# Planning VectorE steps with two SBUF inputs around GpSimd, in the experts of an attention and mixture-of-experts kernel

## The chip, the core and the metric

One core of one Trainium2 chip. The metric is device time in microseconds (us) from the first to the last instruction of one execution, all outputs being written to HBM. Engines are TensorE (PE in the profile's rows), VectorE (DVE), ScalarE (ACT), GpSimd (POOL) and SyncE (SP), which issues the DMAs. Each engine works off its own queue in order.

## What is computed

Clustered attention over 4 batches and 8 heads (768 rows of 64), and a dense mixture of 8 experts on its output, 3072 tokens by 512. Only the second half is touched by the change:

```python
logits = x @ w_gate                      # x: 3072 x 512, 8 experts
P = np.exp(logits - logits.max())
for _ in range(8):                       # rows and columns of P normalised in turn
    ...
for e in range(8):
    h = np.maximum(x @ w1[e], 0.0)       # 512 -> 1024
    out += P[:, e:e+1] * (h @ w2[e])     # 1024 -> 512
```

All is float32 to the outside. The expert products are done in float16 pairs: each operand is split into a high half and the rest, and three products of halves are added up.

## The kernel before

**Stages.** Attention fills the first 490 us. The experts follow, in 64 units of work; a unit is one batch (768 tokens), one expert and one half of that expert's hidden columns, and has two halves of 256 columns each. The first units are (batch 0), (batch 1), (batch 1), (batch 0), then batch 2 twice and batch 3 twice, all of expert 0. So unit 4 is the first that needs the x tiles of batch 2, and unit 6 those of batch 3.

**One half of a unit.** The first layer is a 2x2 block scheme with seven products in place of eight (`layer1`, lines 1493 to 1522), each of six matmuls of 128x384. They are accumulated in three PSUM tiles, `a_ps`, `b_ps` and `c_ps`. In between, partial results are copied out: ScalarE makes `c11`, `c22`, `c12` and `h21` (line 1529, functions `c_11`, `c_22`, `c_12`, `sums_of`), and TensorE's next product into the same PSUM tile waits for that copy: the second product of `a_ps` for c11, the second of `c_ps` (operand B22) for c22, the third of `a_ps` (operand T3) for c12. VectorE then adds the second product from PSUM (line 1532, one SBUF input). From these come seven operands of the second layer: c12, c22 and c11 through a relu (`split_raw`: ScalarE line 1538, VectorE line 1540), and four sums s1, h21, s2 (kept in c22) and s4 (kept in c12), made on VectorE by `relu_with` (line 1623, two SBUF inputs) and split by `split_sum` (ScalarE's cast, line 1547, and a subtraction, line 1549, on GpSimd or VectorE). Each of the tiles c11, c12, c22, h21 and s1 has two buffers; the c22 buffer comes back when s4 has read it and s2 is split, that of c12 when s4 is split.

**Second layer.** `layer2` multiplies the operands with the second weights into three PSUM banks (line 1693), and VectorE adds the results to the accumulators (lines 1727, 1729, 1733). The first three batches are added up for expert 0 without a gate and scaled by it afterwards on ScalarE (line 1744).

**Beside it** run the gates (lines 1195 to 1251, with tiny matmuls, line 1239), the making of the weight operands (`make_first`, lines 1302 to 1321, and `make_second`, lines 1341 to 1360; 4 subtractions and 3 splits each on GpSimd or VectorE), the scan of the next expert's weights for their largest value (line 323 on VectorE, then two DMAs through HBM, lines 274 and 277), and the x tiles of batches 2 and 3 (`next_x`): load (line 1408), for batch 3 a largest value and its round trip, scaling (line 1425), four subtractions (line 338), seven splits (line 1437), store (line 1440) and load for the unit (line 1471).

**The order** is written by a planner in the program (`Planner`, lines 62 to 166). Each piece of work is a generator that yields an engine and a duration before it issues its instructions; the planner keeps a time for each engine, begins the step that can start first (within a patience of 0.1 us the one with the smallest due time), and fixes each engine's order as planned. A step may name two engines, `either` (line 1275), and is then given to the one that can begin first, VectorE with a handicap of 0.3 or 1.5 us. The names in `PORT`, `"POOL"` and `"DVE*"`, share one more time, `self.port`: such a step starts only when the last one of either kind has ended. Attention's steps already use `"DVE*"`; the experts' used plain `DVE`, which knows nothing of GpSimd. The plan's times set the order alone; on the chip semaphores rule.

Of the kernel before, what the change touches and what calls it, by code (L numbers as in the profile page):

```python
# [171 lines left out]
def attn_moe_kernel(  # L172
# [63 lines left out]
    PE, ACT, DVE, POOL, SP = "PE", "ACT", "DVE", "POOL", "SP"  # L236
# [113 lines left out]
    with ExitStack() as actx:  # L350
# [178 lines left out]
        ev = Events()  # L529
# [623 lines left out]
    FULL = NG2 * B  # L1153
# [25 lines left out]
    ev = Events()  # L1179
# [8 lines left out]
    def urgent(t):  # L1188
        plan.now.key = lead + t
# [85 lines left out]
    def either(pool, dve, alone=False):  # L1275
        if alone:
            return (POOL, pool)
        return (POOL, pool), (DVE, dve, 0.3 if ev["slot", FULL].time is None else 1.5)

    def raw_tile():  # L1280
        return rawp.tile([P, 1024], F32, name="raw")
# [5 lines left out]
    def make_first(e, f2):  # L1287
# [18 lines left out]
        for o, a, b_, op in ((0, (0, 0), (0, 1), ALU.add), (1, None, (1, 0), ALU.subtract), (2, (1, 0), (0, 0), ALU.subtract), (3, (1, 1), None, ALU.subtract)):  # L1306
            w = yield either(0.82, 0.4, e == 0 and f2 < 2)
            if o == 0:
                sums = sump.tile([P, 1024], F32, name="sums")
                S_ = sums.rearrange("p (o c f) -> p o c f", o=4, c=KC)  # L1310
            x = S_[:, 0] if a is None else A[:, a[0], a[1]]
            y = S_[:, 1] if b_ is None else A[:, b_[0], b_[1]]
            by(w).tensor_tensor(out=S_[:, o], in0=x, in1=y, op=op)
        yield ACT, 0.4
        t = wa[e, f2] = wap.tile([P, 2, 7, KC, P], F16, name="wa")
        for o, a, cost in ((slice(A22, A22 + 1), A[:, 0, 1:2], 0.4), (slice(A11, A12 + 1), A[:, 1], 0.61), (slice(S1, S4 + 1), S_, 1.04)):
            if cost > 0.4:
                yield ACT, cost
            nc.scalar.copy(t[:, 0, o], a)
            w = yield either(2 * cost, 1.15 * cost, e == 0 and f2 < 2)  # L1320
            by(w).tensor_tensor(out=t[:, 1, o], in0=a, in1=t[:, 0, o], op=ALU.subtract)
# [4 lines left out]
    def make_second(e, f2):  # L1326
# [18 lines left out]
        for o, a, b_, op in ((0, (0, 1), (0, 0), ALU.subtract), (1, None, (1, 1), ALU.subtract), (2, (1, 1), (0, 1), ALU.subtract), (3, (1, 0), None, ALU.add)):  # L1345
            w = yield either(0.82, 0.4, e == 0 and f2 < 2)
            if o == 0:
                sums = sump.tile([P, 1024], F32, name="sums")
                T_ = sums.rearrange("p (o f) -> p o f", o=4)
            x = T_[:, 0] if a is None else Bk[:, a[0], a[1]]  # L1350
            y = T_[:, 1] if b_ is None else Bk[:, b_[0], b_[1]]
            by(w).tensor_tensor(out=T_[:, o], in0=x, in1=y, op=op)
# [171 lines left out]
    def k_tile(k, name):  # L1524
        t = kt[k, name] = cp.tile([P, HB], F32, name=name)
        return t

    def scaled(t, ps, func=AF.Copy):
        nc.scalar.activation(t, ps[:, 0:HB], func, scale=KAPPA)  # L1529
# [4 lines left out]
    def split_raw(k, o, c):  # L1534
        yield t_h
        yield ACT, 0.522
        t = h[k, o] = hp.tile([P, 2, HB], F16, name="h")
        nc.scalar.activation(t[:, 0], c, AF.Relu)  # L1538
        yield DVE, 0.607
        nc.vector.scalar_tensor_tensor(out=t[:, 1], in0=c, scalar=0.0, in1=t[:, 0], op0=ALU.max, op1=ALU.subtract)  # L1540
        ev["h", k, o].set(plan)

    def split_sum(k, o, c):
        yield t_h
        yield ACT, 0.522
        t = h[k, o] = hp.tile([P, 2, HB], F16, name="h")
        nc.scalar.copy(t[:, 0], c)  # L1547
        w = yield either(0.95, 0.54)
        by(w).tensor_tensor(out=t[:, 1], in0=c, in1=t[:, 0], op=ALU.subtract)  # L1549
        ev["h", k, o].set(plan)  # L1550

    def c_12(k, t):
        yield ev["p", k, 2]
        yield t_k["c12"]
        urgent(t + 6)
        yield ACT, 0.49
        c = k_tile(k, "c12")
        scaled(c, ps1[k, "a"])
        ev["u2", k].set(plan)
        yield ev["p", k, 3]  # L1560
        urgent(t + 8)
        yield DVE, 0.555
        plus(c, ps1.pop((k, "c")))
        t_c.put(plan)
        ev["c12", k].set(plan)
        urgent(t + 14)
        yield from split_raw(k, "A12", c)

    def c_22(k, t):
        yield ev["p", k, 1]  # L1570
        yield t_k["c22"]
        urgent(t + 4)
        yield ACT, 0.49
        c = k_tile(k, "c22")
        scaled(c, ps1[k, "c"])
        ev["m5", k].set(plan)
        yield ev["p", k, 4]
        urgent(t + 10)
        yield DVE, 0.555
        plus(c, ps1[k, "a"])  # L1580
        ev["c22", k].set(plan)
        urgent(t + 15)
        yield from split_raw(k, "A11", c)
# [18 lines left out]
    def freed(name, *events):  # L1602
        for x in events:
            yield x
        t_k[name].put(plan)

    def sums_of(k, t):
        yield ev["p", k, 6]
        yield t_k["h21"]
        urgent(t + 14)  # L1610
        yield ACT, 0.49
        h21 = k_tile(k, "h21")
        scaled(h21, ps1.pop((k, "a")), AF.Relu)
        t_a.put(plan)
        yield ev["c11", k]
        yield t_k["s1"]
        urgent(t + 17)
        yield DVE, 0.58
        s_1 = k_tile(k, "s1")
        c11, c12, c22 = (kt[k, n] for n in ("c11", "c12", "c22"))  # L1620

        def relu_with(out_, c, other, op):
            nc.vector.scalar_tensor_tensor(out=out_, in0=c, scalar=0.0, in1=other, op0=ALU.max, op1=op)  # L1623

        relu_with(s_1, c11, h21, ALU.add)
        ev["s1", k].set(plan)
        plan.spawn(freed("c11", ev["s1", k], ev["h", k, "A22"]), lead + t)
        plan.spawn(split_sum(k, "S1", s_1), lead + t + 18)
        urgent(t + 20)
        yield DVE, 0.58  # L1630
        relu_with(h21, c22, h21, ALU.subtract)
        plan.spawn(split_sum(k, "S3", h21), lead + t + 26)
        plan.spawn(freed("h21", ev["h", k, "S3"]), lead + t)
        yield ev["h", k, "A11"]
        urgent(t + 20)
        yield DVE, 0.58
        relu_with(c22, c22, s_1, ALU.subtract)
        ev["s2", k].set(plan)
        plan.spawn(split_sum(k, "S2", c22), lead + t + 22)
        plan.spawn(freed("s1", ev["s2", k], ev["h", k, "S1"]), lead + t)  # L1640
        yield ev["h", k, "A12"]
        urgent(t + 24)
        yield DVE, 0.58
        relu_with(c12, c12, c22, ALU.add)
        ev["s4", k].set(plan)
        plan.spawn(split_sum(k, "S4", c12), lead + t + 28)
        plan.spawn(freed("c22", ev["s4", k], ev["h", k, "S2"]), lead + t)
        plan.spawn(freed("c12", ev["h", k, "S4"]), lead + t)
# [171 lines left out]
```

## Time and profile before

| | us |
|---|---|
| median of 3 runs (2294.29 to 2296.83) | 2295.07 |
| profiled execution: span from first to last instruction | 2294.3 |
| TensorE busy, share of the span | 2233.1, 97% |
| VectorE busy | 1859.2, 81% |
| GpSimd busy | 1408.1, 61% |
| ScalarE busy | 1161.5, 51% |

The page gives no other time for the profiled execution than its span, which agrees with the lowest of the runs. Busy times are summed durations; a VectorE instruction that is held up after its start counts as busy. The page's chain of waits, followed back from the end, is TensorE for 88% of the span, VectorE for 5% and others for the rest. What TensorE waits for stands in the rows below.

### The profile page before, as it was taken

The numbers are of one execution on the slowest core, as the hardware profiler recorded it, in microseconds if no ns is written. First come the engines' busy times: TensorE is split into PE (matmuls) and PEld (weight loads), VectorE is DVE, ScalarE is ACT, GpSimd is POOL, SyncE is SP. The second block draws the span as 40 slices with busy tenths as digits, with TensorE's granted clock in tenths as the row PEclk, the third lists the DMA queues.
The fourth block names the chain that finished last, engine by engine and source line by source line (L and its number), as shares of the span: only waits on it lengthen the run. The fifth ranks groups of instructions, "written<-read, shape, count | busy, mean of one in ns | idle before, by whom it ended". The sixth has DMA issues, their size and how long they took to land.

```text
span 2294.3 us, 43174 instructions
## 1 busy us (share of the span) xinstructions
PE 2233.1 (97%) x16190; PEld 1606.9 (70%) x16190; DVE 1859.2 (81%) x3544; ACT 1161.5 (51%) x2324; POOL 1408.1 (61%) x1385
## 2 busy tenths in 40 slices
PE   7999999988989999999999999999999999999998
PEld 4666666546767777777777777777777777777777
DVE  7887877779977987788779877987797789777776
ACT  4565656656555545454535453545454444445432
POOL 5887878878755756464737473747465655556431
PEclk7999999999999999999999999999999999999999
DMA  7675554544521524152426232523343253414242
GB/s 159 158 164 146 136 139 112 160 165 152 184 91 72 180 79 141 57 189 90 141 64 198 70 115 86 170 79 107 121 137 113 71 162 96 134 49 135 61 138 78
DMA packets 178010, 281.03 MB, mean 122 GB/s; under 512 B 64596, under 2 KB 101384, under 8 KB 177288
## 3 DMA queue, kind: packets, MB, share of 16 engines
q1 hardware_dynamic: 177800, 278.27, 41.3%
q8 instruction: 127, 2.08, 0.4%
q14 instruction: 83, 0.68, 0.1%
HBM read 225.82 MB, written 23.69 MB: 109 GB/s over the span
## 4 chain that ended last, share of the span: by engine, by line
PE 88%; DVE 5%; POOL 2%; ACT 2%; issue 2%; DMA 1%; SPq 0%; DVEq 0%; POOLq 0%; ACTq 0%
PE a_ps L1509 20%; PE a_ps L1693 14%; PE ac_ps L1693 12%; PE c_ps L1693 10%; PE c_ps L1509 10%; PE b_ps L1509 5%; PE av_ps L900 5%; PE max_ps L767 3%; PE exp_ps L838 3%; PE exp_ps L839 2%; DVE mrt L771 1%; PE misc_ps L626 1%; ACT pe L845 1%; PE misc_ps L938 1%; PE misc_ps L662 0%
## 5 line engine op out<-in xcount | busy, mean ns | idle before, releaser
L1693 PEld LDWEIGHTS <-h 128*128 128x128 f16 x8064 | 789.9, 98 | 192.6 <-issue 7.6
L1509 PEld LDWEIGHTS <-wa 128*128 128x128 f16 x5376 | 526.7, 98 | 278.6 <-issue 17.3
L1549 POOL TENSOR_TENSOR h<-s,h 128x384 f16<-128x384 f32 x127 | 124.8, 983 | 541.0 <-ACT h L1547 530.3
L1538 ACT ACTIVATE h<-c 128x384 f16<-128x384 f32 x384 | 200.5, 522 | 437.3 <-DVE c L1532 435.8
L1693 PE MATMUL a_ps<-wb,h 128*128 128x256 f16 x3072 | 377.2, 273 | 0.7 <-DVE acc L1733 0.6
L1693 PE MATMUL ac_ps<-wb,h 128*128 128x256 f16 x2688 | 367.3, 273 | 1.0 <-DVE acc L1729 1.0
L1693 PE MATMUL c_ps<-wb,h 128*128 128x256 f16 x2304 | 284.2, 273 | 3.9 <-DVE acc L1729 2.8
L1733 DVE SCALAR_TENSOR_TENSOR acc<-a_ps,gates,acc 128x256 f32<-128x256 f32 x460 | 215.1, 479 | 88.7 <-PE a_ps L1693 85.9
L867 POOL TENSOR_TENSOR psum<-psum,pe 128x512 f32<-128x512 f32 (+1 forms) x240 | 247.9, 1056 | 43.1 <-ACT pe L845 40.1
L1549 POOL TENSOR_TENSOR h<-c,h 128x384 f16<-128x384 f32 x252 | 249.3, 1001 | 27.6 <-ACT h L1547 26.5
L1540 DVE SCALAR_TENSOR_TENSOR h<-c,h 128x384 f16<-128x384 f32 x384 | 255.2, 668 | 6.8 <-ACT h L1538 6.7
L1733 DVE SCALAR_TENSOR_TENSOR acc<-ac_ps,gates,acc 128x256 f32<-128x256 f32 x402 | 192.2, 478 | 34.0 <-PE ac_ps L1693 31.6
L771 DVE TENSOR_REDUCE mrt<-max_ps 128x1 f32<-128x512 f32 (+1 forms) x288 | 188.5, 683 | 38.1 <-PE max_ps L767 36.5
L1733 DVE SCALAR_TENSOR_TENSOR acc<-c_ps,gates,acc 128x256 f32<-128x256 f32 x344 | 155.8, 477 | 74.9 <-PE c_ps L1693 74.4
L1529 ACT ACTIVATE c<-a_ps 128x384 f32<-128x384 f32 x256 | 125.1, 489 | 162.6 <-PE a_ps L1509 162.4
L845 ACT ACTIVATE pe<-exp_ps 128x512 f32<-128x512 f32 x288 | 166.5, 598 | 68.6 <-PE exp_ps L839 60.2
L1547 ACT CAST h<-c 128x384 f16<-128x384 f32 x256 | 128.2, 509 | 81.4 <-DVE c L1623 81.1
L1549 POOL TENSOR_TENSOR h<-h,h 128x384 f16<-128x384 f32 x124 | 140.4, 1132 | 36.0 <-PE c_ps L1693 23.9
L900 PE MATMUL av_ps<-pe,vn 128*64 128x512 f32 (+1 forms) x768 | 132.7, 491 | 0.0
L767 PE MATMUL max_ps<-kX,qX 96*128 96x256 f32 (+1 forms) x384 | 120.6, 385 | 10.8 <-DVE mrt L771 5.5
L839 PE MATMUL exp_ps<-qX,kX 98*128 98x512 f32 (+1 forms) x384 | 126.1, 340 | 0.0
L1529 ACT ACTIVATE h<-a_ps 128x384 f32<-128x384 f32 x128 | 62.7, 490 | 111.8 <-PE a_ps L1509 111.6
(472 smaller groups left out, 3916.7 us busy)
## 6 DMA issues: line engine op xcount, KB each, us to landing
raw<-in_moe_w SPq DMA_DIRECT2D x120, 512.0 KB
qn<-in_q SPq DMA_DIRECT2D x16, 384.0 KB
kn<-in_k SPq DMA_DIRECT2D x16, 384.0 KB
qX<-qH SPq DMA_DIRECT2D x32, 192.0 KB
kX<-kH SPq DMA_DIRECT2D x32, 192.0 KB
vn<-in_v SPq DMA_DIRECT2D x8, 768.0 KB
xd<-xT SPq DMA_DIRECT2D x4, 1536.0 KB
xqB<-xd SPq DMA_DIRECT2D x16, 384.0 KB
```

The costliest lines, as they stand in the source:

```text
L767: nc.tensor.matmul(ps[:, y * (z - a) : (y + 1) * (z - a)], t["qa"][0:96, i * P : (i + 1) * P], t["k2"][0:96, a:z], start=True, stop=True)
L771: nc.vector.tensor_reduce(out=t["mr"][:, i0 : i0 + ni, ni - 1], in_=ps.rearrange("p (x c) -> p x c", x=ni), axis=AX, op=ALU.max)
L845: nc.scalar.activation(pe, ps.rearrange("p (x c) -> p x c", x=ni), AF.Exp, scale=SCALE)
L867: (nc.gpsimd if w == POOL else nc.vector).tensor_tensor(out=st[:, a:z], in0=old[a], in1=part, op=ALU.add)
L900: nc.tensor.matmul(av[o, a:z], vn[:, i, :], heads[t]["pe", c][:, i - i0], start=(i == 0), stop=False, skip_group_check=True)
L1509: nc.tensor.matmul(ps[:, 0:HB], wt[:, w_, a, c, :], xv[:, x_, c, :], start=(n in (0, 1, 5) and s_ == 0), stop=(s_ == len(steps) - 1), skip ...
L1529: nc.scalar.activation(t, ps[:, 0:HB], func, scale=KAPPA)
L1538: nc.scalar.activation(t[:, 0], c, AF.Relu)
L1540: nc.vector.scalar_tensor_tensor(out=t[:, 1], in0=c, scalar=0.0, in1=t[:, 0], op0=ALU.max, op1=ALU.subtract)
L1549: by(w).tensor_tensor(out=t[:, 1], in0=c, in1=t[:, 0], op=ALU.subtract)
L1693: nc.tensor.matmul(view(m, i), t[:, a_, i * P : (i + 1) * P], w[:, b_, x, :], start=(opens and n == 0 and i in (0, 2)), stop=(n == 5), ski ...
L1733: nc.vector.scalar_tensor_tensor(out=to, in0=src, scalar=gate[b, e][:, ti : ti + 1], in1=to, op0=ALU.mult, op1=ALU.add)
```

## The change

Five places in the experts' plan name `"DVE*"` in place of `DVE`: the two-engine steps of `either`, the VectorE half of `split_raw`, and the four relu sums of `sums_of`. No duration, due time or instruction is altered, but the order of ScalarE, VectorE, GpSimd and SyncE in the experts comes out differently, and the choice between two engines.

```diff
     def either(pool, dve, alone=False):
         if alone:
             return (POOL, pool)
-        return (POOL, pool), (DVE, dve, 0.3 if ev["slot", FULL].time is None else 1.5)
+        return (POOL, pool), ("DVE*", dve, 0.3 if ev["slot", FULL].time is None else 1.5)
...
         nc.scalar.activation(t[:, 0], c, AF.Relu)
-        yield DVE, 0.607
+        yield "DVE*", 0.607
         nc.vector.scalar_tensor_tensor(out=t[:, 1], in0=c, scalar=0.0, in1=t[:, 0], op0=ALU.max, op1=ALU.subtract)
...
         urgent(t + 17)
-        yield DVE, 0.58
+        yield "DVE*", 0.58
         s_1 = k_tile(k, "s1")
...
         urgent(t + 20)
-        yield DVE, 0.58
+        yield "DVE*", 0.58
         relu_with(h21, c22, h21, ALU.subtract)
...
         urgent(t + 20)
-        yield DVE, 0.58
+        yield "DVE*", 0.58
         relu_with(c22, c22, s_1, ALU.subtract)
...
         urgent(t + 24)
-        yield DVE, 0.58
+        yield "DVE*", 0.58
         relu_with(c12, c12, c22, ALU.add)
```

In the whole program 12 steps go from VectorE to GpSimd: nine of line 1549, one each of lines 1313, 1321 and 1437. TensorE's order differs only in where the small matmuls of line 1239 stand.

**Place A, unit 1, first half.** ScalarE, from the copy of c11 to that of c12; numbers tell the buffers apart, and c22_6094, c12_6105 and h21_6149 (below) belong to unit 0's first half. Before:

```order
L1529 ACTIVATE c11_6276<-a_ps_6248 128x384
L1547 CAST h_6281<-s1_6274 128x384
L1529 ACTIVATE c22_6286<-c_ps_6267 128x384
L1538 ACTIVATE h_6291<-c11_6166 128x384
L1302 ACTIVATE raw_6097<-raw_6097,s1_93 128x1024
L1547 CAST h_6301<-c22_6179 128x384
L1547 CAST h_6313<-h21_6257 128x384
L1222 ACTIVATE pr_6015<-lg_80,gneg_6311 128x24x8
L1529 ACTIVATE c12_6317<-a_ps_6248 128x384
```

Now:

```order
L1529 ACTIVATE c11_6279<-a_ps_6240 128x384
L1547 CAST h_6282<-h21_6149 128x384
L1547 CAST h_6292<-c22_6094 128x384
L1547 CAST h_6297<-s1_6294 128x384
L1222 ACTIVATE pr_6015<-lg_80,gneg_6299 128x24x8
L1547 CAST h_6306<-c12_6105 128x384
L1529 ACTIVATE c22_6309<-c_ps_6256 128x384
L1547 CAST h_6324<-h21_6252 128x384
L1425 ACTIVATE xqB11_6250<-xqB11_6250,sx_96 128x768
L1529 ACTIVATE c12_6331<-a_ps_6240 128x384
```

The copies of c22 and c12 now stand behind casts of unit 0's sums. On VectorE these sums come, before the change, in one run:

```order
L1623 SCALAR_TENSOR_TENSOR s1_6164<-c11_6086,h21_6150 128x384
L1623 SCALAR_TENSOR_TENSOR h21_6150<-c22_6094,h21_6150 128x384
L1202 TENSOR_REDUCE gmax_6181<-lg_80 128x1
L1623 SCALAR_TENSOR_TENSOR c22_6094<-c22_6094,s1_6164 128x384
L1623 SCALAR_TENSOR_TENSOR c12_6105<-c12_6105,c22_6094 128x384
```

and now with nine other steps between (these rows and the sum into c12_6105, which follows):

```order
L1623 SCALAR_TENSOR_TENSOR s1_6195<-c11_6086,h21_6149 128x384
L1532 SCALAR_TENSOR_TENSOR c12_6189<-c_ps_6151,c12_6189 128x384
L1532 SCALAR_TENSOR_TENSOR c22_6171<-a_ps_6141,c22_6171 128x384
L1532 SCALAR_TENSOR_TENSOR c11_6165<-b_ps_6212,c11_6165 128x384
L1211 TENSOR_REDUCE g1_6247<-g_ps_6210 1x1
L1540 SCALAR_TENSOR_TENSOR h_6158<-c11_6086,h_6158 128x384
L1623 SCALAR_TENSOR_TENSOR h21_6149<-c22_6094,h21_6149 128x384
L1540 SCALAR_TENSOR_TENSOR h_6219<-c12_6189,h_6219 128x384
L1623 SCALAR_TENSOR_TENSOR c22_6094<-c22_6094,s1_6195 128x384
L1540 SCALAR_TENSOR_TENSOR h_6225<-c22_6171,h_6225 128x384
L1623 SCALAR_TENSOR_TENSOR s1_6294<-c11_6165,h21_6252 128x384
L1219 TENSOR_SCALAR gneg_6299<-g_ps_6271 128x1
```

The sums of unit 0's first half have moved behind the three combinations from PSUM (line 1532) and four other steps of its second half.

**Place B, unit 3, second half** (the first half is alike). ScalarE, from c11 to c12, before:

```order
L1529 ACTIVATE c11_7035<-a_ps_7011 128x384
L1435 CAST xt2T2_7051<-xqB11_6259 128x768
L1529 ACTIVATE c22_7069<-c_ps_7040 128x384
L1547 CAST h_7072<-s1_7049 128x384
L1529 ACTIVATE c12_7088<-a_ps_7011 128x384
```

Now:

```order
L1529 ACTIVATE c11_7188<-a_ps_7173 128x384
L1435 CAST xt2T2_7201<-xqB11_6250 128x768
L1435 CAST xt2B22_7241<-xqB22_6273 128x768
L1547 CAST h_7245<-h21_6967 128x384
L1547 CAST h_7250<-c22_6834 128x384
L1435 CAST xt2T3_7259<-xqB12_6266 128x768
L1547 CAST h_7265<-c12_6858 128x384
L1529 ACTIVATE c22_7267<-c_ps_7194 128x384
L1435 CAST xt2B21_7294<-xqB21_6269 128x768
L1529 ACTIVATE c12_7302<-a_ps_7173 128x384
```

The copy of c22 has moved behind the casts of the earlier half's h21, c22 and c12 and two more tiles of batch 2.

**Place C, unit 4, first half.** ScalarE around the scalings of line 1744. Before, they stand behind the copy of c12 and the splits of its tiles:

```order
L1529 ACTIVATE c22_7449<-c_ps_7428 128x384
L1529 ACTIVATE c12_7474<-a_ps_7392 128x384
L1547 CAST h_7477<-h21_7389 128x384
L1547 CAST h_7489<-c22_7250 128x384
L1547 CAST h_7501<-c12_7274 128x384
L1538 ACTIVATE h_7512<-c12_7474 128x384
L1538 ACTIVATE h_7536<-c22_7449 128x384
L1744 ACTIVATE acc111_6772<-acc111_6772,gates_7534 128x256 x2
L1744 ACTIVATE acc122_6884<-acc122_6884,gates_7534 128x256 x2
```

Now:

```order
L1529 ACTIVATE c22_7471<-c_ps_7413 128x384
L1744 ACTIVATE acc111_6738<-acc111_6738,gates_7476 128x256 x2
L1744 ACTIVATE acc122_6840<-acc122_6840,gates_7476 128x256 x2
L1744 ACTIVATE acc121_7008<-acc121_7008,gates_7476 128x256 x2
L1744 ACTIVATE acc111_6738<-acc111_6738,gates_7476 128x256
L1744 ACTIVATE acc122_6840<-acc122_6840,gates_7476 128x256
L1744 ACTIVATE acc121_7008<-acc121_7008,gates_7476 128x256
L1744 ACTIVATE acc112_6909<-acc112_6909,gates_7476 128x256
L1547 CAST h_7513<-s1_7488 128x384
L1744 ACTIVATE acc112_6909<-acc112_6909,gates_7476 128x256 x2
L1529 ACTIVATE c12_7520<-a_ps_7379 128x384
```

All twelve scalings and a cast of s1 now lie between the copies of c22 and c12.

## Rows read from the trace of the kernel before

**Rows 1.** Busy time of each engine in three stretches (columns in the second line).
```profile
core 0: us, PE busy (x) PEld busy (x) DVE busy (x) ACT busy (x) POOL busy (x), PEclk, DMA share, GB/s
490.00:700.00 210.00, 184.09 (x1310) 129.03 (x1304) 182.16 (x337) 118.47 (x229) 150.28 (x130) 0.95 0.47 162
700.00:2200.00 1500.00, 1500.00 (x11497) 1124.68 (x11495) 1226.49 (x2371) 722.09 (x1435) 858.72 (x827) 1.00 0.36 111
2200.00:2294.00 94.00, 88.44 (x701) 68.33 (x699) 68.06 (x138) 28.75 (x61) 23.06 (x24) 1.00 0.34 110
```

**Rows 2.** TensorE's waits, 500 to 680 us: sum, times, longest (us).
```profile
PE c_ps L1509 <- ACT c L1529: 4.7, 3, 2.7
PE a_ps L1509 <- ACT c L1529: 3.9, 2, 1.9
PE c_ps L1693 <- DVE acc L1729: 2.8, 2, 1.5
PE a_ps L1509 <- DVE c L1532: 2.7, 2, 2.2
PE ac_ps L1693 <- DVE acc L1729: 1.0, 2, 0.6
PE b_ps L1509 <- DMA x4B<-xsd2B: 0.5, 1, 0.5
PE g_ps L1239 <- DVE csum L1234: 0.4, 1, 0.4
```

**Rows 3.** Timeline of TensorE: start, duration, group, [idle before, releaser] (us).
```profile
515.77 1.90 PE L1509 MATMUL c_ps<-xsB,wa 128*128 128x384 f16 x6 [2.68 <-ACT c L1529]
517.46 2.10 PE L1509 MATMUL a_ps<-xsT,wa 128*128 128x384 f16 x6
...
528.58 1.14 PE L1509 MATMUL a_ps<-x1T,wa 128*128 128x384 f16 x6 [1.93 <-ACT c L1529]
...
685.73 1.23 PE L1509 MATMUL a_ps<-x6T,wa 128*128 128x384 f16 x6 [3.67 <-DMA x6T<-xsd3T]
...
692.36 1.15 PE L1509 MATMUL a_ps<-x6T,wa 128*128 128x384 f16 x6 [0.87 <-DMA x6T<-xsd3T]
```

**Rows 4.** Timeline of all engines around 512 us.
```profile
511.94 2.43 POOL L1360 TENSOR_TENSOR wb<-sums,wb 128x1024 f16<-128x1024 f32 x1
...
512.32 2.47 DVE L1623 SCALAR_TENSOR_TENSOR s<-c,h 128x384 f32<-128x384 f32 x1
...
514.82 0.51 ACT L1547 CAST h<-s 128x384 f16<-128x384 f32 x1 [3.15 <-DVE s L1623]
...
515.24 0.48 ACT L1529 ACTIVATE c<-c_ps 128x384 f32<-128x384 f32 x1
```

**Rows 5.** Lines, 490 to 720 us: ns least/median/most; two of the page: busy us, mean ns.
```profile
L1623 DVE SCALAR_TENSOR_TENSOR s<-c,h x13: 541/867/2473, 512.3 to 694.1; 128x384 f32<-128x384 f32 x13
...
L1532 DVE SCALAR_TENSOR_TENSOR c<-b_ps,c x13: 541/546/558, 511.3 to 690.9; 128x384 f32<-128x384 f32 x13
...
L1549 POOL TENSOR_TENSOR h<-c,h x24: 905/935/1237, 518.5 to 699.4; 128x384 f16<-128x384 f32 x24
...
L1360 POOL TENSOR_TENSOR wb<-sums,wb x4: 2131/2282/2727, 511.9 to 579.9; 128x1024 f16<-128x1024 f32 x4
...
L1425 ACT ACTIVATE xqB<-xqB,sx x8: 918/923/935, 535.2 to 644.9; 128x768 f32<-128x768 f32 x8
...
L1437 POOL TENSOR_TENSOR xt2B<-xqB,xt2B x3: 1640/1641/1648, 549.5 to 600.5; 128x768 f16<-128x768 f32 x3
...
L323 DVE TENSOR_REDUCE am<-raw 128x1 f32<-128x1024 f32 x56 | 67.5, 1205 | 0.0
...
L1729 DVE TENSOR_TENSOR acc<-c_ps,acc 128x256 f32<-128x256 f32 x24 | 9.6, 416 | 2.9 <-PE c_ps L1693 2.9
```

**Rows 6.** Timeline of ScalarE near 622 us: the scalings.
```profile
622.10 4.90 ACT L1744 ACTIVATE acc<-acc,gates 128x256 f32<-128x256 f32 x12
```

**Rows 7.** Timeline of GpSimd near 682 us: batch 3's last subtraction.
```profile
681.93 1.80 POOL L338 TENSOR_TENSOR xqB<-xqB,xqB 128x768 f32<-128x768 f32 x1 [0.89 <-DVE xt3B L1437]
```

## The prediction, made before the change was run

> **What bounds the kernel now.** I read first the busy time by stretch, to see where TensorE waits at all. From 700 to 2200 us it is busy 1500.00 of 1500.00 us; from 490 to 700 us, the start of the experts, it stands for 210 − 184.09 = 25.9 us; after 2200 us for 5.6 us, most of it behind the last matmul [rows 1]. Attention, before 490 us, is built instruction for instruction as before. So the change is decided between 490 and 700 us, by what it does to TensorE's waits there: TensorE's own order is the same but for some places of the gates' small matmuls.
>
> Second, who ends those waits. From 500 to 680 us they sum to 4.7 + 3.9 + 2.8 + 2.7 + 1.0 + 0.5 + 0.4 = 16.0 us, nearly all for a ScalarE copy out of PSUM, a VectorE combination or an accumulation [rows 2]. Third, the rows of TensorE: after a wait of 1.93 us a group of six 128x384 matmuls takes 1.14 us; after the wait of 2.68 us two such groups take 1.90 and 2.10, the second nearly twice as long, which is the lower of the clock's two levels, 1.2 GHz [rows 3]. That is 0.76 + 0.96 = 1.7 us lost. So I price a wait above 2 us at 1.7 us more. Last, the end of the start: TensorE waits 3.67 and 0.87 us for batch 3's x tiles (unit 6) [rows 3], whose chain runs from the subtraction on GpSimd at 681.93 to the tile that ends the wait at 692.36 [rows 3, 7]. After that it never waits until the last 25 us.
>
> **What the change does.** No arithmetic changes. The planner lets five kinds of VectorE step start only when GpSimd's planned operation is over, and the reverse. The trace says that the wait is real: the s1 sum took 2.47 us while GpSimd's wb split ran from 511.94 to 514.37 [rows 4], against 0.541 at best; the combination with one PSUM input never took over 0.558 [rows 5]. The Trainium skill says the same (SBUF — State Buffer, section "Who interferes with whom"): a VectorE instruction with two SBUF inputs and a GpSimd instruction that reads SBUF block each other fully, and whoever issues first goes on. By that rule the new plan is the truer one; what it would then give is the first rival.
>
> Twelve steps move from VectorE to GpSimd: nine of L1549 and one each of L1313, L1321 and L1437. An L1549 split takes 0.935 us on GpSimd in the median [rows 5], so with the larger ones some 12 us are added to its 150.28 of 210 us in this stretch [rows 1] if all fell there; no TensorE matmul reads them at once, and I price them at nothing by themselves. What counts is what now stands in front of the copies for which TensorE waits. In the plan a VectorE step that may not start is passed over for one that may, a reduction of a weight tile (L323) or a copy; by then GpSimd has begun again. So the four relu sums (L1623) sink in VectorE's queue, and on ScalarE, whose queue is in order as well, the copies that need a c22 or c12 buffer back sink with them.
>
> **Place A, unit 1, first half.** Nothing differs up to GpSimd's wb split at 511.94. Then ScalarE's copies no longer stand behind the cast of s1, which waits for the 2.47 us sum: c22 is copied by 513.1 instead of 515.7 [rows 4], and TensorE's group of 515.77 can start near 513.6, at full clock: 2.2 + 1.7 = 3.9 us ahead. This is given back. The next c22 copy stands behind the cast of c12, hence behind the c12 sum of unit 0, in front of which VectorE now has three combinations, two small steps and, with it, seven two-input steps after s1: 3 x 0.545 + 0.4 + 7 x 0.55 = 5.9 us, plus four GpSimd operations that come between (two splits and, priced like them, a sum at 0.9 each, and the wb split of at least 2.1 [rows 5]: 4.8). From 515.2 this ends near 526; cast and copy (0.51 + 0.48 [rows 4]) follow, and TensorE, done by 522 with the seven groups of 1.14 [rows 3] that lie between, goes on near 527: a wait of 5 us, and the slow clock. The c12 copy then stands behind the cast of h21 (two sums and four GpSimd steps later, 530.8) and a 0.92 us scaling of x [rows 5]: 532.8, a wait of 3.7 us. So the group that started at 528.58 starts near 533: 4.4 us later, 1.7 more for the clock. Without any GpSimd step between, c22 would be there at 522.5, and A would end some 5 us ahead; I take the full value, because those four steps are queued and ready. A: **+6.1**.
>
> **Between A and B** nothing in the new order blocks a copy. The waits of before there, for ScalarE (1.9), VectorE (0.5 of the 2.7), the accumulations (2.8) and csum (0.4) [rows 2], go: **−5.7**. None of them had a slow clock behind it.
>
> **Place B, unit 3, both halves.** Each time the c22 copy stands behind the casts of c22 and c12, where in the old order it came ahead of both. First half: after the layer-2 group, VectorE does two accumulations of 0.4, the c22 sum, a small reduction and the c12 sum before ScalarE can cast c12 and copy c22: 2 x 0.4 + 3 x 0.55 + 2 x 0.5 = 3.5, and half of a GpSimd split (0.9) whose reading frees the buffer, come to about 4.0 us [rows 4, 5], in which TensorE has no other group. Second half: with a weight tile's reduction of 1.2 us in place of the accumulations and the 1.64 us split of batch 2's x in the way [rows 5], 4.0 + 0.4 + some of the 1.64, up to 5.5 us; 2.5 if the sum slips in ahead of both; I take 3.5, since some of it lies beside a group. Two slow clocks: 3.4. What goes are the waits for x4B (0.5) and for the accumulations into ac_ps (1.0) [rows 2]. B: 10.9 − 1.5 = **+9.4**.
>
> **Place C, unit 4.** Twelve scalings of the accumulators, 4.90 us together [rows 6], stand ahead of a c12 copy for which TensorE's T3 group waits; before, they came behind it, beside TensorE's work. Some 0.9 us of them lie beside a group, a cast and the copy follow (1.0): 5.0 us, and 1.7 for the clock. In exchange the c22 combination now stands ahead of the step that waits for batch 3's maximum, so that the wait of 2.17 goes with its 1.7 us of clock, and the 1.50 of the 4.7 us [rows 2, 3]. C: 6.7 − 5.4 = **+1.3**. Further on three scalings (1.2 us) stand ahead of a c11 copy: **+1.2**.
>
> **Batch 3.** Its steps keep their places against TensorE's groups within a few rows; the last subtraction stands 0.4 us of matmuls later, and 10.4 us lie from it to the loaded tile (681.93 to 692.36) [rows 3, 7]: **+0.4**. From there on nothing waits, as before.
>
> Sum: 6.1 − 5.7 + 9.4 + 1.3 + 1.2 + 0.4 = +12.7 us. The profiled execution spans 2294.3 us, 0.8 below the median of the runs, 2295.07; I forecast **2307 us**. The terms' lower ends (A −5, B 4, C −1, the others as they are) make −6, their upper ends (A 8, B 12, C 3, and half of the 5.7 us kept) +22.
>
> **Rivals.** A difference under 0.2% (4.6 us) can't be told from none here.
>
> *Faster.* If the chip hands VectorE its turn early at A and B, as it did wherever a sum took 0.541 [rows 5], those places cost nothing, and what is saved stands: 3.9 at A, the 5.7 between, 1.5 at B, without C's gain or loss: 11 us, of which batch 3's chain takes back some 4, since its two DMA round trips don't get shorter. That gives about 2288. It decides from the point where the c12 sum of unit 0 is done by 522 instead of 526. For it: the truer plan. Against it: s1 has a median of 0.867 [rows 5], and the copies' places in the queue are fixed. Chance 0.14.
>
> *No change.* TensorE's delay is absorbed by the 3.67 + 0.87 us that it waits for batch 3 anyway [rows 3], if that chain isn't delayed with it. Against it: the chain starts when batch 2's splits are done, and these stand later against TensorE's groups. About 2296. With smaller waits at A and B the sum ends here as well. Chance 0.18.
>
> *Slower still.* Batch 2's splits are planned 10 to 17 us of matmuls later in the middle of the stretch. If unit 4's last tiles then land late, behind the four loads of batch 3 on the same queues (x4B made TensorE wait 0.5 already [rows 2]), 4 to 8 us come on top: 2313. A wait that returned in every unit of the long stretch would cost far more, but VectorE is busy 1226 and GpSimd 859 of its 1500 us [rows 1], and TensorE's order there is unchanged. Chance 0.13, slower too.
>
> My forecast has 0.55. Slower by over 0.2% is then 0.55 + 0.13 = 0.68, no change 0.18, faster 0.14. The range, 2290 to 2320, leaves out the best of the faster cases and the worst of the others.
>
> **What would show it.** In the profile of after: TensorE idle some 35 us between 490 and 712 us instead of 25.9, at a granted clock below the 0.95 of before [rows 1]; waits of 3 to 6 us for c copies (L1529) about 20 and 25 us of work into the experts, two in unit 3 and one of 5 us in unit 4 behind L1744; no wait at 515; unit 6's x tiles still waited for; no wait from 710 to 2200 us. If TensorE waits less than 16 us for copies in all, the walk through A and B is wrong; if it waits in the long stretch, the cover that I took for granted is gone.

## The result and the profile after

The changed kernel takes **2322.09 us** (median of 4 runs, 2319.88 to 2325.56) against 2295.02 before: a ratio of 1.0117, interval 1.0102 to 1.0131, 27 us slower. Slower was forecast, but by 12.7 us; the time lies 2 us above the range. The profiled execution spans 2318.9 us, 24.6 more than that of before. (A run's time is 1.7 to 2.3 us more than its span in all runs below. So the span of before belongs to an execution of about 2296 us, above the median and not the lowest, and that of after to one of 2321.0, below it; hence 24.6 here and 27 there.)

Busy time by stretch, as in [rows 1] (columns in the first line):

```profile
core 0: us, PE busy (x) PEld busy (x) DVE busy (x) ACT busy (x) POOL busy (x), PEclk, DMA share, GB/s
490.00:700.00 210.00, 177.83 (x1223) 123.23 (x1220) 153.42 (x304) 110.91 (x213) 145.04 (x131) 0.90 0.41 138
700.00:2200.00 1500.00, 1491.36 (x11402) 1115.91 (x11401) 1214.42 (x2355) 738.30 (x1434) 809.96 (x830) 1.00 0.36 112
```

From 490 to 700 us TensorE stands for 32.2 us instead of 25.9, at a granted clock of 0.90 instead of 0.95, and after 700 us, where it never waited before, 8.6 us more; 6.4 of these are its waits for batch 3's x tiles, which came before 700 us. VectorE (182.16 to 153.42 us) and GpSimd (150.28 to 145.04) are less busy there. Over the whole program VectorE's busy time falls from 1859.2 to 1835.9 us and GpSimd's from 1408.1 to 1358.9, though GpSimd has twelve steps more. The change did what it says, as two lines of the sums show too (line 1623, ns least/median/most; first the kernel before, whose thirteen start up to 697 us, as do those of [rows 5], then the first thirteen of after):

```profile
L1623 DVE SCALAR_TENSOR_TENSOR c<-c,s x13: 550/1001/1389, 515.9 to 696.8; 128x384 f32<-128x384 f32 x13
...
L1623 DVE SCALAR_TENSOR_TENSOR s<-c,h x13: 540/551/2489, 513.5 to 713.6; 128x384 f32<-128x384 f32 x13
L1623 DVE SCALAR_TENSOR_TENSOR c<-c,s x13: 540/550/1991, 519.7 to 717.5; 128x384 f32<-128x384 f32 x13
```

The median of s1 falls from 867 [rows 5] to 551 ns, that of the sum kept in c22 from 1001 to 550. So the steps wait less for the other engine; TensorE waits more. Its largest waits from 500 to 760 us:

```profile
PE a_ps L1509 <- ACT c L1529: 10.8, 4, 5.0
PE c_ps L1509 <- ACT c L1529: 8.5, 3, 4.2
PE a_ps L1509 <- DMA x6T<-xsd3T: 6.4, 2, 4.6
PE g_ps L1239 <- DVE csum L1234: 4.5, 2, 2.4
```

The waits for ScalarE's copies have grown from 8.6 us [rows 2] to 19.3. The timeline of TensorE shows them at the places named:

```profile
526.45 2.08 PE L1509 MATMUL c_ps<-x1B,wa 128*128 128x384 f16 x6 [4.17 <-ACT c L1529]
...
531.51 2.08 PE L1509 MATMUL a_ps<-x1T,wa 128*128 128x384 f16 x6 [2.75 <-ACT c L1529]
...
583.36 1.47 PE L1693 MATMUL a_ps<-wb,h 128*128 128x256 f16 x12 [1.04 <-DVE acc L1729]
...
590.85 0.39 PE L1239 MATMUL g_ps<-csum,ones 128*128 128x8 f32 x2 [2.11 <-DVE csum L1234]
...
592.61 2.08 PE L1509 MATMUL c_ps<-x3B,wa 128*128 128x384 f16 x6 [1.37 <-ACT c L1529]
...
610.93 0.39 PE L1239 MATMUL g_ps<-csum,ones 128*128 128x8 f32 x2 [2.39 <-DVE csum L1234]
...
614.26 2.08 PE L1509 MATMUL c_ps<-x3B,wa 128*128 128x384 f16 x6 [2.94 <-ACT c L1529]
...
637.88 2.08 PE L1509 MATMUL a_ps<-x4T,wa 128*128 128x384 f16 x6 [5.01 <-ACT c L1529]
...
668.01 2.08 PE L1509 MATMUL a_ps<-x4T,wa 128*128 128x384 f16 x6 [2.65 <-ACT c L1529]
...
711.37 1.67 PE L1509 MATMUL a_ps<-x6T,wa 128*128 128x384 f16 x6 [4.56 <-DMA x6T<-xsd3T]
```

Since TensorE's order is nearly the same, each of its groups can be found in both timelines, and the difference of the two starts says how much had been lost by then. The forecast column gives its terms between the same groups:

| up to | start before, after (us) | behind | of it here | forecast |
|---|---|---|---|---|
| the experts' first groups | 506.11, 507.31 | +1.20 | +1.2 | 0 |
| the wait for s1 is gone | 519.51, 516.42 | −3.09 | −4.3 | −3.9 |
| A done | 536.30, 539.09 | +2.79 | +5.9 | +9.0 |
| between A and B | 582.31, 581.06 | −1.25 | −4.0 | −3.5 |
| B, first half | 598.00, 602.83 | +4.83 | +6.1 | +4.5 |
| B, second half | 613.80, 627.16 | +13.36 | +8.5 | +5.2 |
| C | 647.30, 663.58 | +16.28 | +2.9 | +1.3 |
| the c11 copy behind scalings | 654.50, 673.32 | +18.82 | +2.5 | −0.3 |
| batch 3's x tiles | 694.66, 715.33 | +20.67 | +1.9 | +0.4 |
| unit 9 | 776.87, 799.41 | +22.54 | +1.9 | 0 |
| the end | 2294.3, 2318.9 | +24.6 | +2.1 | 0 |

They differ from those under the prediction's headings, though their sum is the same +12.7: of its −5.7 between A and B, 1.0 us (csum 0.42, the combination 0.54) lies before 536.30 and 1.2 (an accumulation, at 592.64) in unit 3; of the waits that go, the 1.5 us counted at B lie in C's row, and the 1.50 us counted at C in the next.

The first row is not the change's: attention is built alike, and in the fourteen other executions with the same attention below this difference was −0.5 to 3.2.

### The profile page after: what moved, and what is told of

It is laid out like the page before. It is cut to its first block, busy times and chain, and to the rows that moved or that the text cites. A ratio compares the mean times of both kernels' runs of the same rounds, so it can differ in the third digit from the quotient of the medians.

```text
span 2318.9 us, 43218 instructions
## 1 busy us (share of the span) xinstructions
PE 2242.3 (97%) x16190; PEld 1610.7 (69%) x16190; DVE 1835.9 (79%) x3532; ACT 1179.2 (51%) x2324; POOL 1358.9 (59%) x1397
## 4 chain that ended last, share of the span: by engine, by line
PE 88%; DVE 5%; ACT 3%; DMA 2%; POOL 2%; issue 1%; SPq 0%; DVEq 0%; ACTq 0%; POOLq 0%
PE a_ps L1509 21%; PE a_ps L1693 14%; PE ac_ps L1693 12%; PE c_ps L1693 11%; PE c_ps L1509 10%; PE b_ps L1509 5%; PE av_ps L900 5%; PE max_ps L767 3%; PE exp_ps L838 2%; PE exp_ps L839 2%; DVE mrt L771 1%; ACT pe L845 1%; PE misc_ps L626 1%; ACT ot L705 1%; PE misc_ps L938 1%
## 5 line engine op out<-in xcount | busy, mean ns | idle before, releaser
L1549 POOL TENSOR_TENSOR h<-c,h 128x384 f16<-128x384 f32 x256 | 239.4, 937 | 197.0 <-ACT h L1547 152.5
L1733 DVE SCALAR_TENSOR_TENSOR acc<-a_ps,gates,acc 128x256 f32<-128x256 f32 x460 | 208.7, 478 | 93.6 <-PE a_ps L1693 91.7
L1540 DVE SCALAR_TENSOR_TENSOR h<-c,h 128x384 f16<-128x384 f32 x384 | 274.5, 722 | 2.0 <-ACT h L1538 2.0
L1549 POOL TENSOR_TENSOR h<-h,h 128x384 f16<-128x384 f32 x128 | 122.5, 957 | 102.2 <-ACT h L1547 74.8
L1529 ACT ACTIVATE c<-c_ps 128x384 f32<-128x384 f32 x128 | 62.7, 490 | 93.4 <-PE c_ps L1509 83.0
```

The source lines that it names most:

```text
L1733: nc.vector.scalar_tensor_tensor(out=to, in0=src, scalar=gate[b, e][:, ti : ti + 1], in1=to, op0=ALU.mult, op1=ALU.add)
```

## The experiments

Theory S at the start: the relu sums, passed over in VectorE's queue, are what makes the copies late. G: it is the splits that go to GpSimd. O: any other order of this start loses.

**1. Each kind of step alone, and a mere nudge.** The diff edits six lines, of three kinds: one for `either`, one for `split_raw`, four for the sums. The edits are the diff's lines for one kind; the nudge leaves the engine's name and changes a planned duration:

```diff
-        yield DVE, 0.58
+        yield DVE, 0.56
```

> Only the four relu sums (L1623) wait their turn in the plan. Theory S (the sums are passed over in VectorE's queue, so the c22 and c12 buffers come back late and ScalarE's copies with them): most of the loss, 2310 to 2322, with TensorE waiting over 10 us for c copies between 500 and 680 us. Rival G (the loss comes with the splits that go to GpSimd): 2295, within 5. Rival O (any other order of the start loses against the one before, whatever the rule): somewhere between 2303 and 2325, no better and no worse than the other parts.

> Only the two-engine steps wait their turn in the plan. Theory S: 2295, within 5, since the sums keep their places. Rival G (splits go to GpSimd, and batch 2's and 3's tiles come later): 2308 to 2322, with TensorE waiting for x tiles. Rival O: 2303 to 2325.

> Only the VectorE half of split_raw waits its turn in the plan. Theory S: 2295 to 2303; the second and fourth sum wait for these halves, so a small part of the delay may come this way. Rival G: 2295, within 5. Rival O: 2303 to 2325.

> The kernel before, with 0.56 in place of 0.58 us as the planned duration of the four relu sums: no turns, nothing but another order. Theory S and rival G: 2295, within 5. Rival O: 2303 to 2325, with new waits in the start at places of its own.

| | us | ratio (interval) |
|---|---|---|
| sums_only | 2318.84 | 1.0108 (1.0092 to 1.0123) |
| either_only | 2299.64 | 1.0020 (1.0010 to 1.0029) |
| raw_only | 2304.39 | 1.0040 (1.0026 to 1.0055) |
| nudge | 2296.15 | 1.0007 (0.9998 to 1.0017) |

O and G fall. By the times S does well (only raw_only lies outside, 1.4 us above what S allowed); by the trace it does not. The late copies are there with the sums alone: 13.3 us of waits for c copies from 500 to 680 us, where the kernel before has 8.6. (5.47 of them stand in the view as a wait for a load of x, but the c22 copy ended at 528.86 and the group started at 528.91.) But other waits go, and TensorE is only 2.1 us behind at batch 3's tiles (692.36, 694.45). The loss comes later, in waits from 700 us to the end of which the kernel before and the change have 0.6 us each (waits of sums_only):

```profile
PE ac_ps L1693 <- DVE acc L1733: 12.0, 11, 1.5
PE a_ps L1693 <- DVE acc L1733: 3.1, 10, 0.7
```

They return with each expert (0.91 and 1.45 us, at 1047.56 and 1060.91, then at 1270.04 and 1283.40, and so on). So nearly the same time has another cause, and what happens in the start needs more than the sums.

**2. One direction, half a turn, a reservation.** The rule has two halves: VectorE's steps wait for GpSimd, and GpSimd for them. The planner's two places that use the shared time were edited, for example for one way:

```diff
-                    if o[0] in self.PORT:
+                    if o[0] == "DVE*":
                         start = max(start, self.port)
...
-            if cost[0] in self.PORT:
+            if cost[0] == "POOL":
                 self.port = start + cost[1]
```

other_way has the names exchanged, half_port has `0.5 * cost[1]`, and reserve adds that a POOL option starts only after any one-engine `"DVE*"` step of smaller due time that could start within 0.3 us of it.

> The change, but in the plan only the VectorE steps wait for GpSimd; GpSimd waits for nobody. Theory W (VectorE's steps, made to wait in the plan for an idle GpSimd, are passed over; sums, combinations and what follows them come late): 2310 to 2325, with new waits of TensorE for c copies in the first 100 us of the experts, and, as with the sums alone, waits that return in the long stretch. Rival H (it is GpSimd that is held up: splits, weight operands and x tiles come late): 2295 to 2300. Rival B (only both waits together fill the shared time): 2295 to 2303 here and in the next.

> The change, but in the plan only GpSimd waits for the VectorE steps; these wait for nobody. Theory W: 2295 to 2300. Rival H: 2310 to 2325, with TensorE waiting for x tiles and weight operands. Rival B: 2295 to 2303.

> The change, but the plan holds the shared time for only half of each step's duration, both ways. Theory W, whose loss grows with how often VectorE finds GpSimd busy: 2296 to 2306. Rival B: 2295 to 2300, since the shared time is then far from full. Rival H: 2300 to 2310. If the order is late whatever the length of the turn: 2315 or more.

> The change, and in the plan a GpSimd step that is less urgent may not begin while a relu sum or a split_raw half that is more urgent is ready. If the loss came only from VectorE's steps being passed over in favour of less urgent GpSimd work: 2297 to 2305, with no c-copy wait over 2 us in units 1 and 3. If the shared time is simply full in the start (rival B), so that giving it to the one makes the other late: 2318 or more, with x tiles and GpSimd's splits later instead.

2316.78 us (1.0095, 1.0078 to 1.0112), 2331.68 (1.0164, 1.0144 to 1.0184), 2309.30 (1.0065, 1.0050 to 1.0080) and 2328.5 (one run, so no interval). None of these can be read as it stands, since attention is planned by the same class and was reordered too: the experts' group that started at 506.11 in the kernel before came at 512.61, 527.79, 519.29 and 509.76, so 6.5, 21.7, 13.2 and 3.7 us had been lost by then, where unchanged attention differs by −0.5 to 3.2. (In attention, then, weakening the rule cost time in the first three; the fourth can't be told from none.) Beyond that the reservation lost another 19 us by 880 us, with 17.0 us of waits for c copies between 500 and 800: giving the turn to the more urgent VectorE step is no cure. The others were run again with the edit in the experts' planner alone.

> The change with the shared time held for half of each step, in the experts' plan alone (attention keeps its order). The earlier run's trace, counted from the experts' first matmul, shows about no loss. Rival B: 2292 to 2299. Theory W, whose loss grows with the length of the turn: 2300 to 2312. A part of the first run's 14.7 us that was attention's: then the loss here is under 4 us.

> Only VectorE waits for GpSimd, in the experts' plan alone. Theory W: 2307 to 2313 (13 us, the earlier trace counted from the experts' first matmul), with the c-copy waits of 5.6 and 7.6 us again. Rival B: 2295 to 2303.

> Only GpSimd waits for VectorE, in the experts' plan alone. The earlier run's trace, counted from the experts' first matmul, shows a loss of 10 us, with a wait of 5.5 us for batch 2's x tile. If both directions cost by themselves (15.7 one way, 10 the other, 27 together): 2303 to 2308. If GpSimd's direction costs nothing in the experts and the earlier loss was left over from attention: 2294 to 2298.

| | us | ratio (interval) |
|---|---|---|
| half_experts | 2296.29 | 1.0008 (0.9999 to 1.0017) |
| one_way_experts | 2310.77 | 1.0069 (1.0054 to 1.0084) |
| other_way_experts | 2308.14 | 1.0058 (1.0042 to 1.0073) |

Taken off the losses of the first runs, these leave 13.5, 6.5 and 23.3 us as the price of the weaker rule in attention. Each direction costs by itself, 15.7 and 13.8 us, together about the 27 of the change. They cost at different places (TensorE's timeline of one_way_experts, then of other_way_experts):

```profile
590.51 2.08 PE L1511 MATMUL c_ps<-x1B,wa 128*128 128x384 f16 x6 [7.60 <-ACT c L1531]
```

```profile
535.85 0.59 PE L1241 MATMUL g_ps<-csum,ones 128*128 128x8 f32 x2 [4.58 <-DVE csum L1236]
...
631.34 2.08 PE L1511 MATMUL b_ps<-x4B,wa 128*128 128x384 f16 x6 [5.91 <-DMA x4B<-xsd2B]
```

VectorE made to wait brings late copies (19.4 us of waits for them up to 720 us, against 5.2); GpSimd made to wait brings late x tiles and a late gate reduction. Theory W (only VectorE's waiting costs) and rival H (only GpSimd's does) are each half of it. Rival B, that only both together do harm, falls with one_way_experts; but it was right on half a turn, which costs nothing that can be measured. At this one point the loss is far from proportional to the length of the turn.

**3. Are the copies late for want of a buffer?** A third c12 and c22 buffer:

```diff
-    NRAW, NH = 3, 20
+    NRAW, NH = 3, 18
-    t_k = {n: Tokens(2) for n in ("c11", "c12", "c22", "h21", "s1")}
+    t_k = {n: Tokens(3 if n in ("c12", "c22") else 2) for n in ("c11", "c12", "c22", "h21", "s1")}
-        t = kt[k, name] = cp.tile([P, HB], F32, name=name)
+        t = kt[k, name] = cp.tile([P, HB], F32, name=name, bufs=3 if name in ("c12", "c22") else 2)
```

> The change, with a third buffer for c12 and for c22 (in exchange two of the twenty buffers of the split operands). If the loss is that ScalarE's copies find no free c22 or c12 buffer because their sums are late (theory W at places A and B): 2300 to 2310, and the c-copy waits of units 1 and 3 (4.17, 2.75, 1.37, 2.94 us) gone. If VectorE's and GpSimd's work as a whole comes later (rival B, a plan that is too full in the start): 2317 to 2325, with waits for other results, of the second layer's operands or accumulations, in the copies' place.

> The control: the kernel before with the same buffers. All theories: 2292 to 2297; over 2298 would mean that the two missing operand buffers cost something themselves, to be taken off the run above.

With the change 2307.95 us (1.0058, 1.0043 to 1.0073), 14 less than without the buffers; in the kernel before 2294.53 (0.9999, 0.9990 to 1.0009). So about half of the loss goes when the copies find a free buffer. (The whole order is planned anew with the buffers; the control's is too, and it gains nothing.) The c-copy waits of units 1 and 3 are gone but for 1.69 and 1.13 us, and by 594 us TensorE is 8.4 us ahead of the kernel before (593.95, 585.51). It doesn't keep this (its timeline):

```profile
601.77 0.61 PE L1693 MATMUL a_ps<-wb,h 128*128 128x256 f16 x2 [3.91 <-ACT h L1547]
...
629.12 2.10 PE L1509 MATMUL a_ps<-x4T,wa 128*128 128x384 f16 x6 [5.04 <-DMA x4T<-xsd2T]
```

The same late sums are met again as operands of the second layer (3.91 us for a cast behind the sum kept in c22, which VectorE began at 599.82), and then the late x tiles (5.04 us here, 2.40 and 4.15 for batch 3's).

**4. The scalings ahead of the c12 copy (place C).**

```diff
-            urgent(piece_time(u + 2, 0))
+            urgent(piece_time(u + 2, 0) + 60)
```

> The change, with the due time of unit 4's accumulator scalings (L1744) 60 us later, so that in ScalarE's order the copy of c12 comes after one of them and not after twelve. If the scalings are what the wait of 5.01 us there stands behind: that wait goes with its slow clock and the time is 5 to 7 us less than with the change, 2314 to 2318. If the copy would be late anyhow, or the gain is lost again in the wait for batch 3's x tiles: 2320 to 2324.

> The change with the third c12 and c22 buffers and the later scalings, both as in the runs before. If the two causes are separate: 2300 to 2304 (2322 - 14 - 7). If they are the same lateness met at two places, or the x tiles of batches 2 and 3 set the end of the start by then: 2305 to 2309, no better than the buffers alone.

late_scale takes 2314.86 us (1.0090, 1.0076 to 1.0104). Each against its own runs of the kernel before, that is 6.6 us less than the change, and the two intervals just touch. The wait of 5.01 is one of 0.20 (its timeline):

```profile
635.57 1.14 PE L1509 MATMUL a_ps<-x4T,wa 128*128 128x384 f16 x6 [0.20 <-ACT c L1529]
```

With the buffers as well it is 2306.13 us (1.0050, 1.0035 to 1.0065), no better than the buffers alone: the two gains don't add up. TensorE then waits 4.75 us for x4T and 6.9 us in three waits for x6T. That is the second of the two cases expected.

**5. What is left over.**

> The change without the four relu sums: the two-engine steps and split_raw's halves wait their turn. Alone they cost 5 and 10 us. If the parts add up: 2308 to 2312. If the loss grows with how much of the shared time is asked for (rival B): 2312 to 2318, more than the sum. If the sums carry it: 2303 or less.

> The rule in the experts only from unit 8 on; the start is planned as before. If the loss lies in the start, as the offset of TensorE's groups shows (20.7 us of 24.6 by 770 us): 2295 to 2300, with the wait of 1.7 us at unit 9 left. If the long stretch suffers by itself, as with the sums alone: 2305 to 2315. If the rule helps where VectorE has slack: 2290 to 2294.

> Turns held for half of each step in the experts, with the third c12 and c22 buffers. If the buffers give what they gave with full turns (14 us) on top of the half turns' 2296: 2285 to 2290, faster than the kernel before. If batch 2's and batch 3's x tiles set the end of the start, whatever the copies do: 2293 to 2298.

no_sums (two of the three kinds): 2307.34 us (1.0058, 1.0044 to 1.0072), 13.0 more than before; alone they cost 5.1 and 9.8, so these two add up within their intervals. (The sums alone cost 24.3, so the three kinds together don't.) TensorE has 13.9 us of waits for c copies up to 720 us here, the longest 5.79, so copies also come late without sums that wait in the plan. late_turns (`DVE` until unit 8 begins, `"DVE*"` from there): 2299.82 us (1.0023, 1.0014 to 1.0033), 5 us slower; so some 22 of the 27 us are the start's, and the long stretch loses a little too. half_buffers: 2297.15 us (1.0011, 1.0003 to 1.0020), so the buffers give nothing on top of half turns, the second case expected. No version was faster than the kernel before.

## Why the prediction was right and wrong

**What failed, in short.** Place B's second half ("I take 3.5, since some of it lies beside a group") measured 5.9 us of wait; the c11 copy behind scalings ("+1.2") 2.65 and the lower clock; and "from there on nothing waits" 3.9 us. By the table's rows these three and B's first half come to 11.7 us more than forecast, C and batch 3 to 3.1 and attention's chance difference to 1.2, while A and the rows beside it came out 4.1 better. That errors of both signs partly cancel, and the time misses the range by only 2 us, is luck. (The forecast also added its 12.7 us to a span, not to a run's time; that is under 1 us.)

**Right:** the sign, the stretch, the places, and that late copies are the larger part (14 us by the buffers). From 490 to 712 us TensorE stands for 38.6 us, "some 35" in the forecast, at a granted clock of 0.91, below the 0.95 of before. The wait at 515 us went and gave 4.3 us for the forecast 3.9; the waits between A and B gave 4.0 for the 3.5 that lie there.

**Step A was mis-sized, and its working was wrong:** +5.9 after the gain, for a forecast +9.0. The c22 copy did come at 526, by luck, since not for the reason given. I let GpSimd have four turns between VectorE's seven two-input steps. The timeline of all engines shows that it had none until the run broke off:

```profile
518.27 0.54 DVE L1540 SCALAR_TENSOR_TENSOR h<-c,h 128x384 f16<-128x384 f32 x1
518.28 3.64 POOL L1549 TENSOR_TENSOR h<-s,h 128x384 f16<-128x384 f32 x1
...
520.61 0.54 DVE L1623 SCALAR_TENSOR_TENSOR s<-c,h 128x384 f32<-128x384 f32 x1
...
521.08 0.14 DVE L1219 TENSOR_SCALAR gneg<-g_ps 128x1 f32<-128x1 f32 x1
521.14 1.20 DVE L1623 SCALAR_TENSOR_TENSOR c<-c,c 128x384 f32<-128x384 f32 x1
...
522.89 2.12 POOL L1360 TENSOR_TENSOR wb<-sums,wb 128x1024 f16<-128x1024 f32 x1
524.97 0.91 POOL L1549 TENSOR_TENSOR h<-c,h 128x384 f16<-128x384 f32 x1
...
525.90 0.49 ACT L1529 ACTIVATE c<-c_ps 128x384 f32<-128x384 f32 x1 [2.83 <-POOL h L1549]
```

VectorE's sums were done by 522.3. It was GpSimd, held for 3.64 us in a split of 0.91, with a wb split ahead of the next, that gave the c22 buffer back at 525.88. The wait was 4.17 instead of 5, and the c12 copy's 2.75 instead of 3.7.

**Step B was too small:** 14.6 us for 9.7. Its first half's wait was right. In these rows, first of the kernel before and then of the change, the group that waits for the c22 copy starts 3.97 us later than before, and 5.9 us later in the second half (10.71 less the 4.83 already lost):

```profile
588.64 1.14 PE L1509 MATMUL c_ps<-x3B,wa 128*128 128x384 f16 x6
...
603.55 1.14 PE L1509 MATMUL c_ps<-x3B,wa 128*128 128x384 f16 x6
```

```profile
588.78 0.76 DVE L1729 TENSOR_TENSOR acc<-c_ps,acc 128x256 f32<-128x256 f32 x2 [1.65 <-PE c_ps L1693]
...
592.07 0.49 ACT L1529 ACTIVATE c<-c_ps 128x384 f32<-128x384 f32 x1 [0.21 <-POOL h L1549]
592.61 2.08 PE L1509 MATMUL c_ps<-x3B,wa 128*128 128x384 f16 x6 [1.37 <-ACT c L1529]
...
613.72 0.48 ACT L1529 ACTIVATE c<-c_ps 128x384 f32<-128x384 f32 x1
614.26 2.08 PE L1509 MATMUL c_ps<-x3B,wa 128*128 128x384 f16 x6 [2.94 <-ACT c L1529]
```

So the waits are 4.0 for the forecast 4.0, and 5.9 for 3.5. In the first half VectorE stands for 1.65 us in front of two accumulations whose matmuls aren't done, with the sum behind them, as the working had it; this is how a step that is passed over in the plan costs more than its own length on the chip. The gates' small matmuls stand inside both waits (2.11 and 2.39 us for csum) but cost nothing: each copy ended 0.05 or 0.06 us before its group started. Three things were missing. In the second half the h21 sum alone took 1.90 us instead of 0.54 beside a split of batch 2's x, of which I had counted only a part, and the c12 sum, behind a reduction of 1.21, took 1.02 beside another split:

```profile
607.46 1.64 POOL L1437 TENSOR_TENSOR xt2B<-xqB,xt2B 128x768 f16<-128x768 f32 x1
607.62 1.90 DVE L1623 SCALAR_TENSOR_TENSOR h<-c,h 128x384 f32<-128x384 f32 x1
...
611.95 0.91 POOL L1549 TENSOR_TENSOR h<-h,h 128x384 f16<-128x384 f32 x1
612.25 1.02 DVE L1623 SCALAR_TENSOR_TENSOR c<-c,c 128x384 f32<-128x384 f32 x1
```

The lower clock lasted for more than one group: 1.5 us and 2.6 us (the offset right after 592.61 and 614.26), for a forecast 3.4. And the first half has two waits that were not forecast, 1.04 us for an accumulation (583.36) and 0.69 for a VectorE combination (600.55).

**Step C:** the mechanism held. The wait was 5.01 us for a forecast 5.0, but the lower clock after it cost 2.8 us (three groups) instead of 1.7. It stands behind these rows of ScalarE:

```profile
632.13 4.11 ACT L1744 ACTIVATE acc<-acc,gates 128x256 f32<-128x256 f32 x10 [1.40 <-DVE gates L1262]
...
637.36 0.47 ACT L1529 ACTIVATE c<-a_ps 128x384 f32<-128x384 f32 x1
```

The next wait, for the c11 copy of unit 4's second half, was 2.65 us and 1.4 of lower clock, where 1.2 in all was forecast: besides the scalings a cast of batch 3's x stands ahead of it.

```profile
665.56 0.82 ACT L1435 CAST xt3B<-xqB 128x768 f16<-128x768 f32 x1
666.28 1.31 ACT L1744 ACTIVATE acc<-acc,gates 128x256 f32<-128x256 f32 x3
```

**"From there on nothing waits" failed:** 3.9 us are lost after 720 us. Half of it is one collision, in a plan made to have none (timeline at unit 9):

```profile
790.26 2.13 POOL L1360 TENSOR_TENSOR wb<-sums,wb 128x1024 f16<-128x1024 f32 x1 [0.66 <-ACT wb L1358]
790.32 2.48 DVE L1540 SCALAR_TENSOR_TENSOR h<-c,h 128x384 f16<-128x384 f32 x1
...
794.19 1.47 PE L1693 MATMUL c_ps<-wb,h 128*128 128x256 f16 x12 [1.70 <-DVE acc L1733]
```

The plan fixes only the order, so its turns need not hold on the chip: these two steps start 0.06 us apart. What shifted them no run shows.

**The rivals.** "Faster" and "no change" are out. "Faster" named its own sign, the c12 sum of unit 0 done by 522 instead of 526, and the sign came true (521.14 + 1.20); the time did not follow, since the copy waited for GpSimd's split and not for the sum. "Slower still" named batch 2's x tiles: with the change they were not waited for, since TensorE was late itself, but they were the next bound as soon as the copies were helped (x4T 5.04 us in more_buffers). Batch 3's chain itself went as forecast: from its last subtraction to the loaded tile it took 10.3 us (701.10 to 711.37), and that tile came 19.0 us later than before, where TensorE was 18.8 behind already. The 1.9 us of its row are the lower clock behind the one wait of 4.56 us.

What stays open: why the sums alone lose almost nothing in the start and some 22 us in the long stretch; and why half a turn is harmless where each direction alone costs 14 to 16 us. That the start's shared time is full with whole turns and has slack with halves fits both, but no run shows it.

## What to carry to other kernels

A conflict that an in-order queue settles with a short stall (here 0.3 us in the median of s1) may be worth less than the order which a planner gives up to avoid it: before such a rule is added, ask which urgent step will be passed over, which buffers it holds, and who waits for them. The same rule, weakened, cost 6 to 23 us in attention, and added, 27 in the experts, so it is tried by stage. And a run that gives the expected time isn't yet the expected cause: the sums alone cost nearly as much as the whole change, at another place.

## What was not expected of the hardware

A run of six VectorE steps with two SBUF inputs, each starting before the last has ended (starts 0.47 us apart, 0.54 us each), kept GpSimd out for the whole run: its split lasted 3.64 us instead of 0.91 and ended after VectorE had begun a 0.14 us step with one PSUM input; VectorE's next sum then took 1.20. It is no rule that the one who is held out must wait for the run's end. Later in the same trace a GpSimd split that began during the second of three such steps came in ahead of the third:

```profile
703.71 0.55 DVE L1540 SCALAR_TENSOR_TENSOR h<-c,h 128x384 f16<-128x384 f32 x1
703.85 1.90 POOL L1437 TENSOR_TENSOR xt3T<-xqB,xt3T 128x768 f16<-128x768 f32 x1 [0.94 <-ACT xt3T L1435]
...
704.18 1.99 DVE L1623 SCALAR_TENSOR_TENSOR c<-c,s 128x384 f32<-128x384 f32 x1
```

What decides between the two stays open. The Trainium skill (SBUF — State Buffer, section "Who interferes with whom") says that whoever issues first has the shared ports for the whole instruction. The second place agrees; in the first, the split was issued 0.45 us ahead of VectorE's second step (518.28, 518.73) and still came in behind all six.
